# An attention kernel with a written-out step list: five score blocks for queries 0 to 255, longer rows for q and k of group 1, and a new list

## The chip, the cores and the metric

The kernel runs on one core of a Trainium2 chip. The core has five engines that run side by side, each on its own list of instructions in order: TensorE (PE) for matmuls and weight loads, VectorE (DVE), ScalarE (ACT) and GpSimd (POOL) for elementwise work, and SyncE (SP), which here only issues transfers. Sixteen DMA engines move data between main memory and the on-chip memory SBUF. Matmuls write into PSUM, a small memory that the kernel cuts into four slots. The metric is the device time of one execution in microseconds.

## The reference

The input is q, k and v of 8 batches, 8 heads, 576 positions and 64 features. First comes attention in a window: a query sees the keys at most 32 positions away.

```python
scores = scale * np.matmul(q, k.transpose(0, 1, 3, 2))
mask = np.abs(pos[:, None] - pos[None, :]) <= 32
attn = softmax(np.where(mask, scores, -1e9))
x = np.matmul(attn, v)                      # heads side by side: (8, 576, 512)
```

Then comes a mixture of four attention experts on x. A gate picks the two best experts for each row and weighs them. Each expert has its own 64-wide wq, wk, wv and wo; its attention is causal.

```python
logits = x @ w_gate                          # top 2 of 4, softmax over the two
for e in range(4):
    a = causal_softmax(scale * (x @ wq[e]) @ (x @ wk[e]).T)
    out += weight[e] * (a @ (x @ wv[e]) @ wo[e])
```

All inputs and the output are float32.

## The kernel before, in words

A batch is done in two groups of four heads; group g of batch b has the number i = 2b + g, from 0 to 15. The work is cut into steps with names, and the string ORDER lists all of them in the order in which their instructions are issued. Each engine takes its own instructions of this list in that order; waits between engines follow from the data and from the four PSUM slots (the digits behind a colon). The numbers of costs and dependencies in the `step(...)` calls served to find the list; when the kernel is built only the list counts.

The steps are:

- `load.i.kn.n`, `load.i.qn.n` bring k or q of group i to SBUF, in float32: four transfers on SP, one for each head, with rows of 768 B (three positions of 64 features). For group 0 each is cut into two halves (n = 0, 1), and its q goes over ACT's queue (L132). Three buffers of each kind are there, so load i waits for the turn of i - 3.
- `turn.i.kn.n`, `turn.i.qn.n` transpose on DVE in blocks of 32 x 32, six instructions each (L289); features come to lie on partitions, 32 for each head, in two halves.
- `S.i.half` is the window's scores (L305): half 0 for queries 0 to 255, half 1 for 256 to 575. BLK lists the blocks as (first of 64 keys, first query, last query + 1), each done for two feature halves and four heads. ACT then takes the exponential (L310), and a mask product sets what lies outside the window to zero (L312), on DVE for groups 0 and 1 and on POOL for the others. A float32 matmul is two matmuls and two weight loads for PE, so a half with 48 matmuls has 192 PE instructions.
- `loadv.b.n` loads v in pieces that overlap by 64 rows; `dup.b.n.m` copies halves of them on ACT or POOL.
- `U.i.x` and `E.b` multiply by v (L332, L343); DVE divides by the sums (L321, L322). `T.b.g` and `TE.b` transpose the result on PE (L354, L363); ACT copies it out (L357, L364) and POOL makes a bf16 copy (L358, L366).
- `G1.b`, `G3.b` are the gate. `QK.b.j.n`, `V.b.p` are the experts' projections (L425, L441), `PS.b.j.c` the causal scores with exponential and mask (L458, L461, L465), `AV.b.j` the product with v (L482), `PT.b.j` a transpose (L499), `Y.b.t` the output projection (L509), its copy on ACT (L514) and its store on SP (L516, L518).
- `WL.*`, `WC.*` load and cast the weights. `w18:2` means 18 warm-up matmuls into slot 2 (L229), whose result nobody uses; ACT reads one column of it (L230).

The list goes through the groups in a pipeline: scores of later groups stand between the experts' steps of earlier batches. It ends with AV, PT and Y of batches 6 and 7.

Of the kernel before, what the change touches and what calls it, by code (L numbers as in the profile page):

```python
# [19 lines left out]
PE = mybir.EngineType.PE  # L20

ORDER = """
    load.0.kn.0 load.0.qn.0 load.1.qn.0 turn.0.kn.0 loadv.0.0 turn.0.qn.0 load.0.qn.1 late.0 load.1.kn.0
    dup.0.0.0 turn.1.qn.0 dup.0.0.3 load.0.kn.1 w18:2 S.0.0:01 loadv.0.1 turn.0.qn.1 turn.1.kn.0 turn.0.kn.1
    w38:2 S.1.0:10 S.0.1:23 load.2.kn.0 dup.0.0.2 turn.2.kn.0 load.3.qn.0 WL.v load.2.qn.0 w4:1 S.1.1:20
    dup.0.1.3 dup.0.0.1 dup.0.1.2 dup.0.1.0 U.0.1:3 U.0.0:2 dup.0.1.1 WL.q U.1.0:0 U.1.1:3 E.0:2 WC.v
    turn.2.qn.0 T.0.0:0 turn.3.qn.0 T.0.1:3 TE.0:2 w8:1 S.2.0:23 load.3.kn.0 V.0.0:0 G1.0:3 WC.q turn.3.kn.0
    S.2.1:02 QK.0.0.0:1 S.3.0:20 QK.0.0.1:1 loadv.1.0 load.4.kn.0 QK.0.1.0:2 load.4.qn.0 G3.0 dup.1.0.3
    PS.0.0.0:1 dup.1.0.2 V.0.1:0 dup.1.0.0 QK.0.1.1:2 dup.1.0.1 PS.0.0.1:1 S.3.1:03 turn.4.kn.0 U.3.0:2
    turn.4.qn.0 PS.0.0.2:1 U.2.0:0 PS.0.1.0:3 U.2.1:2 load.6.qn.0 S.4.0:31 PS.0.1.1:0 E.1:2 load.5.qn.0  # L30
    U.3.1:3 PS.0.0.3:2 PS.0.1.2:0 turn.5.qn.0 TE.1:1 load.5.kn.0 T.1.0:2 T.1.1:3 turn.5.kn.0 S.4.1:10
    loadv.2.0 AV.0.0:2 PS.0.1.3:3 load.6.kn.0 G1.1:1 turn.6.qn.0 S.5.0:30 QK.1.0.0:2 V.1.0:3 dup.2.0.0 G3.1
    dup.2.0.1 dup.2.0.3 QK.1.1.0:2 dup.2.0.2 QK.1.0.1:0 S.5.1:23 turn.6.kn.0 PS.1.0.0:0 QK.1.1.1:1 loadv.3.0
    V.1.1:2 AV.0.1:3 S.6.0:10 U.4.1:2 load.7.kn.0 dup.3.0.0 U.4.0:1 dup.3.0.2 E.2:0 dup.3.0.1 load.7.qn.0
    PS.1.0.1:2 WL.o PT.0.0:3 turn.7.kn.0 T.2.0:1 dup.3.0.3 turn.7.qn.0 S.6.1:30 U.5.1:2 PS.1.1.0:3
    load.8.qn.0 PS.1.0.2:1 U.5.0:0 S.7.0:23 TE.2:1 T.2.1:0 load.8.kn.0 load.9.qn.0 turn.8.qn.0 PS.1.1.1:2
    U.6.0:3 U.6.1:1 WC.o PS.1.0.3:2 PS.1.1.2:0 turn.8.kn.0 G1.2:3 S.7.1:12 G3.2 QK.2.0.0:0 V.2.0:1
    turn.9.qn.0 PS.1.1.3:0 S.8.0:32 loadv.4.0 QK.2.0.1:0 dup.4.0.0 QK.2.1.0:3 load.10.qn.0 U.7.1:2 E.3:3
    dup.4.0.1 U.7.0:0 dup.4.0.3 load.9.kn.0 dup.4.0.2 turn.9.kn.0 PS.2.0.0:2 S.8.1:31 load.11.kn.0 V.2.1:0
    load.10.kn.0 QK.2.1.1:2 PS.2.0.1:3 S.9.0:10 load.11.qn.0 PT.0.1:2 AV.1.0:3 TE.3:2 turn.10.qn.0  # L40
    PS.2.0.2:0 Y.0.0:1 T.3.0:2 turn.10.kn.0 S.9.1:30 PS.2.1.0:1 AV.1.1:2 T.3.1:3 U.8.1:0 load.13.qn.0
    PS.2.1.1:1 turn.11.qn.0 PS.2.0.3:2 G1.3:3 S.10.0:01 load.13.kn.0 QK.3.0.0:2 PT.1.0:0 load.12.kn.0 G3.3
    Y.0.2:1 QK.3.0.1:2 turn.11.kn.0 PS.2.1.2:0 S.10.1:13 V.3.0:2 PS.2.1.3:3 PS.3.0.0:1 U.8.0:0 E.4:3
    load.12.qn.0 PS.3.0.1:1 loadv.5.0 turn.12.qn.0 V.3.1:2 QK.3.1.0:0 S.11.0:13 turn.12.kn.0 QK.3.1.1:0
    AV.2.0:1 Y.0.4:3 PS.3.0.2:2 U.9.0:0 dup.5.0.2 dup.5.0.3 U.9.1:3 S.11.1:12 PT.1.1:3 T.4.1:0 AV.2.1:3
    load.14.kn.0 TE.4:2 T.4.0:1 PT.2.0:2 Y.1.0:0 PS.3.0.3:3 PS.3.1.0:1 G1.4:2 S.12.0:30 G3.4 QK.4.0.0:1
    Y.1.2:3 PT.2.1:0 dup.5.0.0 QK.4.0.1:1 dup.5.0.1 AV.3.0:0 PS.3.1.1:3 PS.4.0.0:1 V.4.0:2 PS.3.1.2:0
    PS.4.0.1:1 U.11.0:3 U.11.1:0 loadv.6.0 U.10.0:1 E.5:3 U.10.1:0 PS.3.1.3:1 PS.4.0.2:3 Y.1.4:2 Y.2.0:1
    V.4.1:3 turn.13.qn.0 QK.4.1.0:2 S.12.1:13 PS.4.0.3:2 QK.4.1.1:0 Y.2.2:1 PT.3.0:2 TE.5:0 turn.13.kn.0
    load.14.qn.0 T.5.0:3 AV.3.1:1 T.5.1:0 PS.4.1.0:3 AV.4.0:2 loadv.7.0 turn.14.kn.0 S.13.0:10 dup.6.0.3  # L50
    QK.5.0.0:3 PS.4.1.1:1 Y.2.4:0 PT.3.1:2 QK.5.0.1:3 PS.4.1.2:2 turn.14.qn.0 load.15.qn.0 S.13.1:01 Y.3.0:3
    V.5.0:2 PS.4.1.3:3 dup.6.0.1 PS.5.0.0:1 dup.6.0.0 G1.5:0 S.14.0:23 QK.5.1.0:1 G3.5 dup.6.0.2 V.5.1:2
    Y.3.2:3 QK.5.1.1:1 PS.5.0.1:2 dup.7.0.1 AV.4.1:0 PS.5.1.0:1 PS.5.0.2:2 U.12.0:3 dup.7.0.0 U.13.1:1
    load.15.kn.0 E.6:2 U.13.0:3 U.12.1:1 PS.5.0.3:2 PS.5.1.1:0 TE.6:3 T.6.1:2 PT.4.0:1 turn.15.kn.0 T.6.0:0
    PS.5.1.2:1 S.14.1:23 dup.7.0.2 turn.15.qn.0 AV.5.0:0 QK.6.0.0:1 PT.4.1:3 V.6.0:2 PS.5.1.3:3 S.15.0:10
    Y.3.4:3 QK.6.1.0:2 QK.6.0.1:0 dup.7.0.3 V.6.1:2 QK.6.1.1:3 PS.6.0.0:0 S.15.1:21 G1.6:3 PS.6.1.0:2
    PS.6.0.1:0 U.14.0:1 U.14.1:2 U.15.0:0 G3.6 U.15.1:1 E.7:2 PS.6.0.2:0 Y.4.0:3 T.7.0:1 TE.7:0 T.7.1:2
    PT.5.0:3 AV.5.1:1 PS.6.1.1:3 PS.6.0.3:0 G1.7:2 PS.6.1.2:3 Y.4.2:0 G3.7 QK.7.0.0:1 AV.6.0:3 PS.6.1.3:0
    QK.7.0.1:1 QK.7.1.0:0 Y.4.4:3 PT.5.1:2 PS.7.0.0:1 QK.7.1.1:0 Y.5.0:2 PS.7.0.1:1 PS.7.1.0:0 V.7.0:3
    PS.7.0.2:1 PT.6.0:2 AV.6.1:0 PS.7.1.1:3 Y.5.2:2 PS.7.0.3:1 PS.7.1.2:3 V.7.1:0 PT.6.1:2 AV.7.0:0  # L60
    PS.7.1.3:2 Y.5.4:3 AV.7.1:0 Y.6.0:3 PT.7.0:2 PT.7.1:2 Y.7.0:2 Y.6.2:0 Y.7.2:0 Y.6.4:2 Y.7.4:2
"""


MASKS = ["DVE"] * 2 + ["POOL"] * 14
DUP = ["ACT", "POOL", "ACT", "POOL"]

S = 576
# [6 lines left out]
def kernel(  # L75
# [43 lines left out]
    def parts(i):  # L119
        return [(0, 3), (3, 6)] if i < 1 else [(0, 6)]  # L120

    def load(b, g, nm, n):

        src = {"kn": k, "qn": q}[nm]
        if n == 0:
            nat[nm, b, g] = natp.tile([128, 6, 3, 64], F32, name=nm, tag=nm)
        t = nat[nm, b, g]
        i = 2 * b + g
        a0, a1 = parts(i)[n]
        eng = nc.scalar if i == 0 and nm == "qn" else nc.sync  # L130
        for hh in range(4):
            eng.dma_start(t[32 * hh:32 * hh + 32, a0:a1, :, :].rearrange("p a s d -> p a (s d)"),  # L132
                          src[b, 4 * g + hh].rearrange("(a p s) d -> p a (s d)", p=32, s=3)[:, a0:a1])


# [124 lines left out]
    def cast_weights(n):  # L260
# [4 lines left out]
        else:  # L265
# [2 lines left out]

    BLK = [[[(128, 64, 192), (64, 0, 128)], [(0, 0, 64), (192, 128, 192)], [(256, 192, 256), (192, 192, 256)]],
           [[(384, 320, 448), (320, 256, 384)], [(512, 448, 576), (448, 384, 512)],
            [(256, 256, 320), (576, 512, 576)]]]
    CUT = [0, 256, 576]
# [5 lines left out]
    def turn(b, g, nm, n):  # L280
        if n == 0:
            qt_[b, g, nm] = (KTS[(2 * b + g) % 2][:, :, 32:608] if nm == "kn" else
                             qkt.tile([128, 2, S], F32, name="T" + nm, tag="T" + nm))
        T = qt_[b, g, nm]
        n_ = nat[nm, b, g]
        a0, a1 = parts(2 * b + g)[n]
        for dh in range(2):
            for x in range(3):
                nc.vector.transpose(T[:, dh, :].rearrange("q (a p s) -> q s a p", p=32, s=3)[:, x, a0:a1],  # L289
                                    n_[:, a0:a1, x, 32 * dh:32 * dh + 32])  # L290

    def win_scores(b, g, half):
        QT, KT = qt_[b, g, "qn"], KTS[(2 * b + g) % 2]
# [234 lines left out]
    def step(name, fn, pe, after, ops=(), slots=()):  # L528
        steps[name] = dict(fn=fn, pe=pe, after=list(after), ops=list(ops), slots=list(slots))

    for b in range(B):
        for g in range(2):
            i = 2 * b + g
            np_ = len(parts(i))
            for nm in ("kn", "qn"):
                for n, (a0, a1) in enumerate(parts(i)):
                    step(("load", i, nm, n), lambda b=b, g=g, nm=nm, n=n: load(b, g, nm, n), 0,
                         [("turn", i - 3, nm, m) for m in range(len(parts(i - 3)))] if i > 2 else
                         [("load", i, nm, 0)] if n else [],
                         [("AQ" if i == 0 and nm == "qn" else "SP", 1.8, -1), ("DMA", 2.3 * (a1 - a0) / 6, 0),  # L540
                          ("LAT", 0.8, 1)])
                    step(("turn", i, nm, n), lambda b=b, g=g, nm=nm, n=n: turn(b, g, nm, n), 0,
                         [("load", i, nm, n)] + ([("turn", i, nm, 0)] if n else []) +
                         ([("S", i - 2, 1)] if i > 1 else []), [("DVE", 0.3 + 1.3 * (a1 - a0) / 6, -1)])
            mk = ("DVE", 0.62) if MASKS[i] == "DVE" else ("POOL", 1.25)
            for half in range(2):
                step(("S", i, half), lambda b=b, g=g, half=half: win_scores(b, g, half), (0.9, 1.1)[half],
                     [("turn", i, nm, n) for nm in ("kn", "qn") for n in range(np_ if half else 1)] + ([("S", i, 0)] if half else []) +
                     ([("U", i - 3, 0), ("U", i - 3, 1), ("E", (i - 3) // 2)] if i > 2 else []),
                     [("ACT", (0.5, 0.6)[half], -1), (*mk, 0), ("ACT", (0.5, 0.6)[half], -1), (*mk, 2)], (0, 2))  # L550
# [114 lines left out]
```

## Time and profile before

| what | value |
|---|---|
| median of 13 runs | 269.7 us (266.84 to 274.45) |
| profiled execution, time | 267.08 us |
| profiled execution, span from first to last instruction | 265.4 us |
| PE busy | 238.6 us (90%), 5940 matmuls, 5940 weight loads |
| DVE, ACT, POOL busy | 171.1, 160.3, 147.5 us |
| mean granted PE clock | 0.993 |
| moved by DMA | 40.72 MB, mean 153 GB/s |
| warm-up matmuls | 68 in four steps (18, 38, 4, 8), PE busy 19.1 us |

The profile names lines of the kernel before with L. In a row of the timeline stand the start in us, the length, the engine, the line, the operation, what it writes and reads, the tile's shape and a count, since neighbours of one kind are merged; in brackets stands how long the engine had been idle before it, and what ended that idle time. "issue" means that nothing in the profile ended it. The row of the DMA queue gives the number of packets, their megabytes and their share of the 16 DMA engines' time; the queue named "instruction" on q8 brings the PE's own instructions. Busy PE time is modelled at its ends, so I go by the starts of steps where a step's length matters.

### The profile page before, as it was taken

Reading aid. Unit: us, or ns where it says so; the run is one execution under the profiler, and the core shown is the slowest. Engines: PE = TensorE matmul, PEld = TensorE weight load, DVE = VectorE, ACT = ScalarE, POOL = GpSimd, SP = SyncE. Lnnn points to the kernel's source line nnn. Section 1 sums busy time; section 2 is a strip of 40 time slices with the busy share of each in tenths; the row PEclk is TensorE's granted clock in tenths of the full one; section 3 lists DMA queues with packets and bytes.
Section 4 is the critical chain, followed back from the end, with each engine's and each line's share of the span. In section 5 each row is a group of like instructions: output and inputs, shape, how many; then the busy total and the mean of one; then the engine's idle time right before and its main releaser. Section 6 shows DMA issues by size and latency. Waiting matters only on the chain. (4 is left out here: it accounts for less than half of the span.)

```text
span 265.4 us, 13457 instructions
## 1 busy us (share of the span) xinstructions
PE 238.6 (90%) x5940; PEld 182.9 (69%) x5940; DVE 171.1 (64%) x538; ACT 160.3 (60%) x247; POOL 147.5 (56%) x202
## 2 busy tenths in 40 slices
PE   7598698988879989878999999999999999999752
PEld 2345686777768778766878877787679878876520
DVE  7554786476757948656968756768558846574530
ACT  1304536677455966556775668577796845867543
POOL 8102035966965997649674775267972974521300
PEclk9989999999999999999999999999999999999999
DMA  6989889999999769941889525639836010223227
GB/s 161 214 181 200 184 198 201 227 211 192 196 213 223 165 143 205 205 84 40 226 214 197 141 84 137 129 101 236 204 103 172 2 25 2 82 83 103 99 111 245
DMA packets 76570, 40.72 MB, mean 153 GB/s; under 512 B 47072, under 2 KB 71648, under 8 KB 76512
## 3 DMA queue, kind: packets, MB, share of 16 engines
q1 hardware_dynamic: 75616, 39.28, 65.2%
q8 instruction: 46, 0.75, 1.3%
q10 hardware_dynamic: 896, 0.59, 0.9%
q14 instruction: 12, 0.10, 0.2%
HBM read 30.42 MB, written 9.44 MB: 150 GB/s over the span
## 5 line engine op out<-in xcount | busy, mean ns | idle before, releaser
L312 POOL TENSOR_TENSOR AT<-AT,MASKP 128x512 f32<-128x512 f32 (+1 forms) x56 | 77.7, 1409 | 38.3 <-ACT AT L310 38.1
L461 ACT ACTIVATE ATE<-ps 128x1024 bf16<-128x1024 f32 (+1 forms) x64 | 52.0, 836 | 22.5 <-PE ps L458 22.1
L310 ACT ACTIVATE AT<-sc 128x512 f32<-128x512 f32 (+1 forms) x64 | 38.2, 650 | 33.7 <-PE sc L305 33.7
L305 PE MATMUL sc<-Tqn,KT 32*64 32x128 f32 (+1 forms) x3072 | 49.5, 255 | 4.4 <-issue 4.0
L305 PEld LDWEIGHTS sc<-Tqn,KT 32*64 32x64 f32 x3072 | 44.0, 130 | 12.3 <-issue 8.4
L332 PE MATMUL u<-VS,AT 128*64 128x65 f32 x1024 | 35.3, 224 | 3.9 <-issue 3.7
L332 PEld LDWEIGHTS u<-VS,AT 128*64 128x64 f32 x1024 | 32.3, 138 | 7.1 <-issue 5.9
L289 DVE STREAM_TRANSPOSE Tqn<-qn 128x192 f32<-128x192 f32 (+1 forms) x102 | 29.0, 392 | 3.1 <-DMA qn<-in_q_dram 3.1
L289 DVE STREAM_TRANSPOSE KT<-kn 128x192 f32<-128x192 f32 (+1 forms) x102 | 29.1, 393 | 2.5 <-DMA kn<-in_k_dram 2.5
L465 POOL TENSOR_SCALAR_AFFINE_SELECT ATE<-ATE 128x384 bf16<-128x384 bf16 x32 | 15.9, 521 | 25.4 <-ACT ATE L461 25.3
L514 ACT COPY ysb<-py 128x1024 f32<-128x1024 f32 (+1 forms) x24 | 20.5, 867 | 10.8 <-PE py L509 8.9
L322 DVE TENSOR_TENSOR XN<-u,rs 128x512 f32<-128x512 f32 (+1 forms) x40 | 25.5, 638 | 1.4
L358 POOL CAST XTB<-XTF 128x512 bf16<-128x512 f32 x32 | 18.6, 614 | 13.9 <-ACT XTF L357 13.7
L161 POOL COPY VS<-VS 64x1024 f32<-64x1024 f32 (+1 forms) x18 | 16.9, 940 | 14.4 <-DMA VS<-in_v_dram 13.8
L509 PE MATMUL py<-WO,OTT 128*128 128x512 bf16 x80 | 20.8, 380 | 2.9 <-ACT ysb L514 2.4
L229 PE MATMUL warm<-WARM 128*128 128x512 bf16 x68 | 19.1, 445 | 4.1 <-ACT wsink L230 2.7
L425 PE MATMUL pp<-XTB,WQ 128*128 128x288 bf16 x128 | 18.7, 287 | 2.4 <-issue 2.4
L357 ACT COPY XTF<-tx 128x512 f32<-128x512 f32 x32 | 17.0, 595 | 6.0 <-PE tx L354 5.6
L441 PE MATMUL pv<-WV,XTB 128*128 128x256 bf16 x160 | 20.1, 273 | 0.2 <-DVE OE L491 0.2
L432 DVE CAST QKE<-pp 128x576 bf16<-128x576 f32 x16 | 12.0, 753 | 12.5 <-PE pp L425 12.5
L458 PE MATMUL ps<-QKE 64*128 64x64 bf16 (+4 forms) x192 | 19.7, 279 | 0.1
L159 ACT COPY VS<-VS 64x1024 f32<-64x1024 f32 (+1 forms) x18 | 17.1, 948 | 3.9 <-DMA VS<-in_v_dram 3.6
(77 smaller groups left out, 314.1 us busy)
## 6 DMA issues: line engine op xcount, KB each, us to landing
qn<-in_q_dram SPq DMA_DIRECT2D x60, 144.0 KB, 4.8
kn<-in_k_dram SPq DMA_DIRECT2D x60, 144.0 KB, 5.0
out_dram<-ysb SPq DMA_DIRECT2D x16, 512.0 KB, 3.1
VS<-in_v_dram SPq DMA_DIRECT2D x21, 256.0 KB, 5.8
VS<-in_v_dram SPq DMA_DIRECT2D x14, 192.0 KB, 5.5
out_dram<-ysb SPq DMA_DIRECT2D x8, 128.0 KB, 2.3
VS<-in_v_dram SPq DMA_DIRECT2D x6, 128.0 KB, 3.3
qn<-in_q_dram ACTq DMA_DIRECT2D x8, 72.0 KB, 3.0
```

What stands on the lines that cost most here:

```text
L229: nc.tensor.matmul(w, WARM[:, 0:128], WARM, start=True, stop=True)
L289: nc.vector.transpose(T[:, dh, :].rearrange("q (a p s) -> q s a p", p=32, s=3)[:, x, a0:a1], n_[:, a0:a1, x, 32 * dh:32 * dh + 32])
L305: nc.tensor.matmul(sl[hh // 2][p0:p0 + 64, hh % 2, lo - c0:hi - c0], KT[r, dh, k0:k0 + 64], QT[r, dh, lo:hi], start=(dh == 0), stop=(dh == ...
L310: nc.scalar.activation(ap, sl[p][:, :, 0:c1 - c0], EXP, scale=scale_att)
L312: eng.tensor_tensor(out=ap, in0=ap, in1=MASK[:, None, c0:c1].to_broadcast([128, 2, c1 - c0]), op=MULT)
L322: nc.vector.tensor_tensor(out=o, in0=u[:, :, :, 0:64], in1=rs[:, :, :, None].to_broadcast([128, n, 4, 64]), op=MULT)
L332: nc.tensor.matmul(us[64 * y:64 * y + 64, t, 65 * hh:65 * hh + 65], A[:, hh, 64 * a:64 * a + 64], V[:, a, 4 * g + hh, 0:65], start=True, s ...
L441: nc.tensor.matmul(o, XTB[:, dt, 128 * t:128 * t + 128], WV[:, dt, :], start=(dt == 0), stop=(dt == NDT - 1))
L458: nc.tensor.matmul(ps[:, eo, at:at + hi - lo], QKE[r, 1, 128 * kt:128 * kt + 128], QKE[r, 0, lo:hi], start=True, stop=True)
L461: nc.scalar.activation(ATE[0:rows, :, 512 * c:512 * c + w], ps[0:rows, :, 0:w], EXP, scale=scale_moe)
L509: nc.tensor.matmul(py[:, t - t0, :], OTT[:, j, 128 * t:128 * t + 128], WO[:, j, :], start=(j == 0), stop=(j == 1))
L514: nc.scalar.copy(ysb[0:n, 0:m, :], py[0:n, 0:m, :])
```

## The change

Three things are changed at once. First, half 0 of the scores has five blocks of keys: the block of keys 192 to 255 took queries 128 to 191 and, apart from them, 192 to 255; now it takes queries 128 to 255 in one. That makes 40 matmuls instead of 48, over the same columns.

```diff
-    BLK = [[[(128, 64, 192), (64, 0, 128)], [(0, 0, 64), (192, 128, 192)], [(256, 192, 256), (192, 192, 256)]],
+    BLK = [[[(128, 64, 192), (64, 0, 128)], [(0, 0, 64), (192, 128, 256)], [(256, 192, 256)]],
```

Second, group 1 loads q and k with one transfer each on SP: a partition gets 18 neighbouring positions of a head, 4608 B in a row. The turn then is two transposes of 128x576 instead of six of 128x192.

```diff
+LONG = range(1, 2)
...
-            nat[nm, b, g] = natp.tile([128, 6, 3, 64], F32, name=nm, tag=nm)
+            nat[nm, b, g] = natp.tile([128, 18, 64], F32, name=nm, tag=nm)
...
+        if i in LONG:
+            nc.sync.dma_start(t, src[b, 4 * g:4 * g + 4].rearrange("h (p s) d -> (h p) s d", s=18))
+            return
...
+            if 2 * b + g in LONG:
+                nc.vector.transpose(T[:, dh, :].rearrange("q (p s) -> q s p", s=18), n_[:, :, 32 * dh:32 * dh + 32])
+                continue
```

Third, the whole list ORDER is another one; it came from a model of the engines that also counts fetches of 256 instructions. The steps are the same but for the warm-ups: 33 in six steps (18, 3, 1, 3, 1, 7) instead of 68 in four. Its beginning, before and after, and some later places of the new one:

```diff
-    load.0.kn.0 load.0.qn.0 load.1.qn.0 turn.0.kn.0 loadv.0.0 turn.0.qn.0 load.0.qn.1 late.0 load.1.kn.0
-    dup.0.0.0 turn.1.qn.0 dup.0.0.3 load.0.kn.1 w18:2 S.0.0:01 loadv.0.1 turn.0.qn.1 turn.1.kn.0 turn.0.kn.1
-    w38:2 S.1.0:10 S.0.1:23 load.2.kn.0 dup.0.0.2 turn.2.kn.0 load.3.qn.0 WL.v load.2.qn.0 w4:1 S.1.1:20
-    dup.0.1.3 dup.0.0.1 dup.0.1.2 dup.0.1.0 U.0.1:3 U.0.0:2 dup.0.1.1 WL.q U.1.0:0 U.1.1:3 E.0:2 WC.v
-    turn.2.qn.0 T.0.0:0 turn.3.qn.0 T.0.1:3 TE.0:2 w8:1 S.2.0:23 load.3.kn.0 V.0.0:0 G1.0:3 WC.q turn.3.kn.0
-    S.2.1:02 QK.0.0.0:1 S.3.0:20 QK.0.0.1:1 loadv.1.0 load.4.kn.0 QK.0.1.0:2 load.4.qn.0 G3.0 dup.1.0.3
+    load.1.kn.0 load.0.qn.0 load.0.kn.0 load.1.qn.0 load.0.qn.1 turn.0.qn.0 turn.1.kn.0 turn.0.kn.0
+    turn.1.qn.0 w18:3 S.0.0:01 loadv.0.0 turn.0.qn.1 load.0.kn.1 dup.0.0.1 dup.0.0.2 turn.0.kn.1 dup.0.0.3
+    dup.0.0.0 w3:3 S.1.0:02 U.0.0:1 S.0.1:20 load.2.kn.0 loadv.0.1 load.2.qn.0 late.0 dup.0.1.1 dup.0.1.3
+    S.1.1:31 turn.2.kn.0 dup.0.1.0 dup.0.1.2 w1:2 U.0.1:0 WL.q w3:2 U.1.0:1 WL.v E.0:3 load.3.qn.0 U.1.1:2
+    T.0.0:0 w1:1 T.0.1:2 turn.2.qn.0 load.3.kn.0 TE.0:0 loadv.1.0 S.2.0:31 w7:0 G1.0:1 turn.3.qn.0
+    turn.3.kn.0 WC.q QK.0.0.0:3 G3.0 load.4.qn.0 S.2.1:02 QK.0.1.0:3 WC.v QK.0.0.1:0 S.3.0:32 PS.0.0.0:0
...
+    load.6.kn.0 turn.5.kn.0 S.4.1:03 AV.0.0:1 dup.2.0.1 QK.1.0.0:2 V.1.0:3 load.8.kn.0 turn.6.qn.0
...
+    S.7.0:01 dup.3.0.3 load.9.kn.0 dup.3.0.2 loadv.4.0 turn.8.qn.0 AV.1.0:2 Y.0.0:3 load.11.kn.0 QK.2.0.0:1
+    V.2.1:0 turn.9.kn.0 G1.2:2 PS.2.0.0:0 S.8.0:13 QK.2.1.1:0 G3.2 PS.2.0.1:1 load.9.qn.0 U.6.1:3 U.6.0:0
...
+    PT.1.1:2 AV.2.0:0 PS.2.1.2:3 S.9.0:12 turn.10.qn.0 V.3.0:3 Y.0.4:2 QK.3.0.0:1 PS.2.1.3:2 S.10.0:30
+    S.9.1:21 PT.2.0:0 QK.3.0.1:3 loadv.5.0 G1.3:0 PS.3.0.0:3 QK.3.1.0:1 dup.4.0.3 G3.3 Y.1.0:2 V.3.1:3
...
+    G1.5:0 S.13.0:23 G3.5 AV.4.0:1 QK.5.0.0:2 load.15.qn.0 load.15.kn.0 Y.2.2:3 V.5.0:0 PS.4.1.3:3 S.12.1:12
...
+    dup.7.0.0 dup.7.0.3 PS.5.1.3:0 PS.6.0.0:1 V.6.0:2 Y.3.4:3 QK.6.1.0:1 PS.6.0.1:3 S.15.1:20 S.14.1:31
```

So load.8.kn, load.9.kn and load.11.kn now come ahead of load.9.qn. The last eight steps, from Y.6.0 to Y.7.4, stand in the order that they had.

## The prediction

> **What bounds the kernel now.** I read three views in this order: busy time by stretch, the timeline around TensorE's (PE's) gaps, and the page's list of DMA queues. The stretches (window, length, then busy us and instruction count of PE, weight loads, DVE, ACT, POOL; last the granted clock, the DMA share, GB/s):
>
> ```profile
> 10.00:15.00 5.00, 3.42 (x10) 1.29 (x10) 3.87 (x14) 1.77 (x4) 0.17 (x1) 0.74 1.07 198
> 28.36:44.63 16.27, 14.46 (x415) 12.30 (x410) 11.49 (x32) 9.09 (x17) 5.13 (x7) 1.00 0.98 198
> 44.63:116.00 71.37, 63.23 (x1921) 51.95 (x1917) 49.69 (x157) 45.55 (x69) 52.93 (x58) 1.00 0.98 197
> 116.00:248.66 132.66, 130.57 (x3110) 102.91 (x3110) 88.50 (x274) 93.17 (x139) 79.35 (x107) 1.00 0.45 117
> ```
>
> From 28 to 249 us PE is the bound. Its steps stand back to back, and what idle time remains is "issue", a wait for nothing that the profile shows. Until 116 us the DMA engines are full too (0.98): a second limit right behind the first. The start is different:
>
> ```profile
> 9.80 1.75 DVE L289 STREAM_TRANSPOSE Tqn<-qn 128x192 f32<-128x192 f32 x6 [2.15 <-DMA qn<-in_q_dram]
> 11.59 10.05 PE L229 MATMUL warm<-WARM 128*128 128x512 bf16 x38 [2.74 <-ACT wsink L230]
> 16.75 2.69 DVE L289 STREAM_TRANSPOSE KT<-kn 128x192 f32<-128x192 f32 x12 [2.37 <-DMA kn<-in_k_dram]
> 21.56 2.75 PE L305 MATMUL sc<-Tqn,KT 32*64 32x128 f32 x192
> ...
> 113.29 1.35 PE L305 MATMUL sc<-Tqn,KT 32*64 32x128 f32 x82
> 115.99 0.37 PE L305 MATMUL sc<-Tqn,KT 32*64 32x64 f32 x14 [1.35 <-issue]
> ```
>
> Here the reader sees that S.1.0 starts only at 21.56: load.1.kn lands at 16.7, and the 38 warm-ups, which themselves waited 2.74 us for their slot, run until 21.6. The last two rows show one score step cut in two by a gap. Its cause:
>
> ```profile
> q8 instruction: 46, 0.75, 1.3%
> ```
>
> The page has 5940 matmuls and 5940 weight loads; 46 fetches make some 256 instructions each. I counted: every such gap stands a multiple of 256 PE instructions from the others. Where 256 instructions are used up in less than about 4.4 us PE stands still until the next block is there (26.91 to 31.28, 111.54 to 115.99); a score step has 192 in 1.4 us. From 44.6 us on these gaps add up to 13.5 us: 8.0 until 97 us, 3.7 until 121, 1.8 later, where a block takes some 3.9 us (DMA 0.45).
>
> **Part 1, the start.** The first stretch is one chain, redone for the new order. DVE starts turns at 5.4, as before, since its memsets end then. Six 96-column transposes take 1.1 us, six of 192 columns 1.75. The two 128x576 ones of a long row are not in the trace: as many elements as six of 192, so from 1.5 (per-column slope of the two rows) to 2.5 (6 x 0.41, the mean of one); I take 2.0. Rows of 4608 B aren't there either: between the rate of 768 B packets (median 51 ns on 16 engines, 240 GB/s) and of 2048 B ones (85 ns, 385 GB/s); I take the longer rows, so 1.18 MB go in 3.1 us instead of 4.9. turn.0.qn.0 ends at 6.5, turn.1.kn 8.5, turn.0.kn.0 9.6: S.0.0 runs at 9.6, 2.2 later than now. turn.1.qn ends at 11.6: S.1.0 at 11.7, not 21.6. Masks (1.3) and both half-turns of block 0 (1.1 each) put S.0.1 at 15.4, the DVE's U.0.0 puts S.1.1 at 17.6; S.1.1 crosses a fetch boundary 4.4 us after the one in S.0.1 and ends at 21.0, against 28.4. U.0.1, w3, U.1.0, E.0, U.1.1 and one more fetch wait: 25.6. T.0.0, T.0.1 (behind 0.9 us of DVE), TE to 28; S.2.0 behind turn.2.qn on DVE, 28.5 to 29.7; w7 1.7, G1.0 1.2; QK.0.0.0 waits for four 0.63 us casts on ACT, which stand behind S.2.0's exponentials: 33.4, against 44.6. V.0.0 (1.85) and S.2.1 (1.48), done by then in the old order, are still owed: 44.6 - 33.4 - 3.3 = **7.9 us** gained. The warm-ups (68 to 33) are worth nothing beyond this: they only filled that wait.
>
> Against it: fewer warm-ups. After 2.8 us of idle PE the clock row above is 0.74, and warm-ups stand 0.425 us apart for a while, then half that. The Trainium skill, "TensorE: Matmul & The Clock Gate", Part 1, says that one idle window of about 3.4 us halves the clock until an equally long busy one. By the rule PE, with waits of 1 to 3 us between short steps until 17.6, could stay at half speed to about 21 us; by the row the cold time was 3.4 us once. Most of the cold work lies under DVE waits; on the path are S.1.1 and U.0.1. Cost 0 to 2.5; I take 1.0. The start then gains **6.9**.
>
> **Part 2, five blocks.** Half 0 has 40 matmuls instead of 48, that is 160 PE instructions, not 192; columns stay 512 per head. A half 0 step takes 1.38 us, half 1 with the same 192 instructions and 640 columns 1.48: so 128 columns cost 0.10, the rest is per instruction: (1.38 - 0.40)/192 = 5.1 ns, times 32 = **0.16 us**. Bounds 0 and 1.38/6 = 0.23. Thirteen such steps lie after QK.0.0.0: six before S.9.0 (1.0), seven after (1.1). ACT and masks are untouched.
>
> **Part 3, the order against the fetches.** I laid the new list on blocks of 256 with the step times of this trace. Blocks under 4.4 us up to about 97 us lack 6.4 us (8.0 measured): 1.6 gained; to 121 us 2.0 (3.7): 1.7 gained. Later it places dense steps together, S.10.0 with S.9.1 (a block of 1.96 us), AV.4.0 with S.13.0 (2.88), S.15.1 with S.14.1 (2.16): at 3.9 us a block, 6.5 missing against 1.8 measured: 4.7 lost. After 97 us the net is **3.0 lost**. The skill's "Runtime: NRT & Kernel Launch", Instruction fetch mechanics, speaks against the whole part: it calls the crossing of a block "mostly hidden", since instructions issue slower than blocks arrive. By the rule this term is 0; the rows (1.35 us idle inside one step) decide against it.
>
> **Part 4, the second limit.** Up to 97 us PE would be ahead by 6.9 + 1.0 + 1.6 = 9.5 us, but the transfers must keep pace. All that goes up to load.4 (q, k, v and weights, 9.8 MB) passes at 197 GB/s from 1.7 us: 51.6 now, 49.8 with the 1.8 us of the long rows. With 1.3 us from landing to the turn (the least that rows show in the start), and 1.8 for the turn, S.4.0 can't run before 52.9; now it is at 59.1, with 0.6 us less to do ahead of it in the new list. So the gain there is at most 5.6, and a blocked turn blocks DVE's copies behind it, and so PE's slots. I take **6.0**: 3.5 are lost to loads. SP's list is moved too: load.8.kn, 9.kn and 11.kn now stand ahead of load.9.qn; by the same sum (19.8 MB ahead of it, at 197 GB/s) it lands at about 105, some 9 us before S.9.0 needs its turn, so it costs nothing more.
>
> **Sum.** 6.0 (up to 97 us) + 1.1 - 3.0 = 4.1 us. The end (AV.7.0 to the last store, 17 us, waits on DVE and ACT) keeps its order: 0. Profiled execution 267.1 -> 263.0; it lies 2.6 under the median of 269.7, so the median goes to **265.6 us**.
>
> **Rivals.** (a) The loads keep pace, because landings now have more slack than the single rows show (load.6.qn and load.3.qn are turned 12 to 18 us after landing): 9.5 + 1.1 - 3.0 = 7.6, 262.1 us. For it: DVE waited for no load after 17 us. (b) The long rows are no faster and the loads leave a gain of 3 only: 3 + 1.1 - 3.0 = 1.1, 268.6 us, no change. For it: DMA 0.98 in the stretch. (c) Slower: fetches. With PE pressed closer against full queues each block takes 4.7 us, also late: the new list then lacks 24.7 us, 11.2 more than the 13.5 measured, of which at most 3.5 lie under load waits: 7.6 - 11.2 = -3.6, 273.3 us. It decides from about 4.5 us a block at the late boundaries. For it: single blocks took 4.9 (to 74.3 us); against: with DMA at 0.45 three stalled ones took 3.8 to 4.3. (d) That it doesn't do what it says is out: the changed list has 40 matmuls in half 0 and single DMAs for load.1.
>
> **Numbers.** Forecast 0.45, (a) 0.27, (b) 0.13, (c) 0.15. A measurement tells 0.5% (1.3 us) from no change. Forecast and (a) are faster but for a twentieth: faster 0.73, same 0.13, slower 0.14. Range: unknown costs (clock 0 to 2.5, blocks 0 to 0.23 each, loads 0 to 3.5) reach from 260 to 269; with part of (c) 259.5 to 270.5.
>
> **What would show it.** S.1.0 at 12 us and QK.0.0.0 near 33 confirm part 1; score steps of half 0 at 1.22 us part 2; gaps inside S.9.1, AV.4.0 and S.14.1 part 3; DVE waiting for kn and qn between 45 and 70 us part 4. Wrong: S.1.0 after 16 us, clock under 1 past 25 us, or more than 20 us of issue gaps.

## The result, and the profile after

The changed kernel takes 264.64 us (median of 11 runs, 263.07 to 270.56); the kernel before, run again beside it, 270.57 us (48 runs). The ratio is **0.9843, 95% interval 0.9807 to 0.9878**: 4.2 us faster (3.3 to 5.2), where 4.1 were forecast. Both kernels have some runs that are several us slower, at a lower granted clock (0.969 against 0.981 on average for the changed kernel); the ratio leaves them out, so it shows less than the two medians. The profiled execution of the changed kernel took 266.54 us (span 264.8), above its median, while that of the kernel before (267.08) lies below its own. So the two traces together show 0.6 us of the gain; they tell where time went, not how much was won.

The same stretches of the changed kernel (columns as before):

```profile
10.00:15.00 5.00, 4.18 (x136) 2.89 (x143) 4.64 (x13) 1.92 (x4) 0.77 (x1) 0.66 1.24 220
28.36:44.63 16.27, 14.76 (x380) 10.95 (x377) 9.83 (x35) 10.19 (x21) 8.29 (x10) 1.00 0.96 191
44.63:116.00 71.37, 64.05 (x1777) 52.04 (x1776) 50.16 (x154) 47.28 (x69) 51.32 (x59) 0.98 0.98 203
116.00:248.66 132.66, 126.51 (x2949) 100.29 (x2948) 86.06 (x268) 88.97 (x134) 78.61 (x106) 1.00 0.45 112
```

The reader is to see the last row: after 116 us PE was busy for 130.57 us of 132.66 before, now for 126.51. It idles 4 us more in a stretch where the DMA engines are busy for only 0.45. In the rows of 28 to 116 us it idles a little less. The start, from the timeline:

```profile
0.80 0.40 SPq L133 DMA_DIRECT2D kn<-in_k_dram  x1
1.26 5.28 SPq L138 DMA_DIRECT2D kn<-in_k_dram  x4
...
8.06 2.30 DVE L295 STREAM_TRANSPOSE KT<-kn 128x576 f32<-128x576 f32 x2
11.51 2.34 DVE L295 STREAM_TRANSPOSE Tqn<-qn 128x576 f32<-128x576 f32 x2 [0.26 <-DMA qn<-in_q_dram]
...
10.82 2.16 PE L314 MATMUL sc<-Tqn,KT 32*64 32x128 f32 x80 [2.50 <-DVE KT L298]
14.22 1.33 PE L314 MATMUL sc<-Tqn,KT 32*64 32x128 f32 x80
...
22.42 1.03 PE L314 MATMUL sc<-Tqn,KT 32*64 32x128 f32 x56 [1.09 <-issue]
```

S.1.0 now runs at 14.22 instead of 21.56, and the step QK.0.0.0 at 36.04 instead of 44.63. It is a real gain, but 2.6 us less than forecast. And two of the gaps of the later part:

```profile
62.08 0.87 PE L491 MATMUL po<-VE,ATE 128*128 128x65 bf16 x23
64.82 0.39 PE L491 MATMUL po<-VE,ATE 128*128 128x65 bf16 x7 [1.87 <-issue]
...
127.78 2.31 PE L314 MATMUL sc<-Tqn,KT 32*64 32x128 f32 x150
131.86 0.47 PE L314 MATMUL sc<-Tqn,KT 32*64 32x64 f32 x26 [1.76 <-issue]
```

AV.0.0 and S.9.1 are cut in two, with "issue" as the reason. Between the two cuts lie 3328 records of PE, its semaphore waits counted in: 13 x 256. So these are instructions that are not there yet. q8 has two fetches fewer than before:

```profile
q8 instruction: 44, 0.72, 1.3%
```

I count such gaps in every trace in one way: the time from one weight load's start to the next right at a multiple of 256 PE instructions (the same multiples as before), where it is over 0.3 us, less the 0.05 us that lie between any two, and without the last 20 us, where PE waits for other engines.

### The profile page after: what moved, and what is told of

Read it like the earlier page. It is cut to its first block, busy times and chain, and to the rows that moved or that the text cites. A ratio compares the mean times of both kernels' runs of the same rounds, so it can differ in the third digit from the quotient of the medians.

```text
span 264.8 us, 12861 instructions
## 1 busy us (share of the span) xinstructions
PE 232.3 (88%) x5649; PEld 179.6 (68%) x5649; DVE 171.6 (65%) x530; ACT 161.5 (61%) x249; POOL 148.6 (56%) x202
## 5 line engine op out<-in xcount | busy, mean ns | idle before, releaser
L314 PE MATMUL sc<-Tqn,KT 32*64 32x128 f32 (+1 forms) x2816 | 49.0, 265 | 10.8 <-DVE KT L298 5.1
L314 PEld LDWEIGHTS sc<-Tqn,KT 32*64 32x64 f32 x2816 | 43.1, 132 | 18.8 <-issue 9.7
L341 PE MATMUL u<-VS,AT 128*64 128x65 f32 x1024 | 35.9, 224 | 4.3 <-issue 3.3
L298 DVE STREAM_TRANSPOSE Tqn<-qn 128x192 f32<-128x192 f32 (+1 forms) x96 | 27.4, 387 | 4.1 <-DMA qn<-in_q_dram 2.2
L523 ACT COPY ysb<-py 128x1024 f32<-128x1024 f32 (+1 forms) x24 | 20.6, 869 | 14.4 <-PE py L518 12.2
L298 DVE STREAM_TRANSPOSE KT<-kn 128x192 f32<-128x192 f32 (+1 forms) x96 | 27.5, 391 | 1.1 <-DMA kn<-in_k_dram 1.0
L474 POOL TENSOR_SCALAR_AFFINE_SELECT ATE<-ATE 128x384 bf16<-128x384 bf16 x32 | 15.9, 521 | 18.9 <-ACT ATE L470 18.7
L167 POOL COPY VS<-VS 64x1024 f32<-64x1024 f32 (+1 forms) x18 | 17.7, 986 | 12.8 <-DMA VS<-in_v_dram 12.3
L367 POOL CAST XTB<-XTF 128x512 bf16<-128x512 f32 x32 | 18.5, 614 | 11.3 <-ACT XTF L366 11.3
L491 PE MATMUL po<-VE,ATE 128*128 128x65 bf16 x480 | 18.2, 193 | 4.8 <-issue 3.0
L450 PE MATMUL pv<-WV,XTB 128*128 128x256 bf16 x160 | 21.1, 281 | 0.1
L491 PEld LDWEIGHTS <-ATE 128*128 128x128 bf16 x480 | 16.2, 97 | 7.2 <-issue 6.9
L441 DVE CAST QKE<-pp 128x576 bf16<-128x576 f32 x16 | 12.1, 754 | 10.8 <-PE pp L434 10.7
```

What stands on the lines that cost most here:

```text
L314: nc.tensor.matmul(sl[hh // 2][p0:p0 + 64, hh % 2, lo - c0:hi - c0], KT[r, dh, k0:k0 + 64], QT[r, dh, lo:hi], start=(dh == 0), stop=(dh == ...
L341: nc.tensor.matmul(us[64 * y:64 * y + 64, t, 65 * hh:65 * hh + 65], A[:, hh, 64 * a:64 * a + 64], V[:, a, 4 * g + hh, 0:65], start=True, s ...
L450: nc.tensor.matmul(o, XTB[:, dt, 128 * t:128 * t + 128], WV[:, dt, :], start=(dt == 0), stop=(dt == NDT - 1))
L491: nc.tensor.matmul(po[:, eo, 65 * qt:65 * qt + 65], ATE[:, eo, o:o + 128], VE[:, kt, 2 * j + eo, :], start=(kt == 0), stop=(kt == qt))
L523: nc.scalar.copy(ysb[0:n, 0:m, :], py[0:n, 0:m, :])
```

## The experiments

All kernels ran beside the kernel before on the same chip. Ratios are to it; the gaps are those of the one profiled execution, in us.

| kernel | ratio (95% interval) | gaps to 44 us | 44 to 118 | after 118 |
|---|---|---|---|---|
| before | 1 | 3.5 | 10.8 | 3.0 |
| changed | 0.9843 (0.9807 to 0.9878) | 1.4 | 8.0 | 7.1 |
| changed, again | 0.9881 (0.9790 to 0.9972) | 1.3 | 6.5 | 7.0 |
| new list alone | 0.9991 (0.9953 to 1.0029) | 2.1 | 9.3 | 6.6 |
| five blocks alone | 0.9853 (0.9772 to 0.9934) | 3.4 | 10.2 | 3.6 |
| five blocks alone, again | 0.9900 (0.9834 to 0.9965) | 2.3 | 11.3 | 2.5 |
| changed without long rows | 0.9896 (0.9848 to 0.9944) | 1.1 | 7.2 | 5.7 |
| changed, shifted by 128 | 0.9859 (0.9796 to 0.9922) | 4.5 | 8.1 | 6.0 |
| changed, few transfers | 0.9436 (0.9367 to 0.9505) | 1.7 | 3.1 | 3.7 |
| before, few transfers | 0.9574 (0.9463 to 0.9686) | 4.3 | 5.1 | 0.9 |
| changed, long rows 1 to 7 | 0.9771 (0.9699 to 0.9844) | 1.9 | 5.4 | 6.9 |
| changed, k of group 0 first | 0.9809 (0.9718 to 0.9901) | 1.3 | 8.0 | 6.0 |
| long rows 1 to 15, k of 0 first | 0.9938 (0.9870 to 1.0007) | 1.9 | 8.3 | 6.5 |
| long rows 1 to 7, k of 0 first, shifted by 64 | 0.9776 (0.9714 to 0.9839) | 2.6 | 7.5 | 1.0 |

### Each part alone

The new list alone is the changed kernel with six blocks and short rows:

```diff
-LONG = range(1, 2)
+LONG = range(0, 0)
...
-    BLK = [[[(128, 64, 192), (64, 0, 128)], [(0, 0, 64), (192, 128, 256)], [(256, 192, 256)]],
+    BLK = [[[(128, 64, 192), (64, 0, 128)], [(0, 0, 64), (192, 128, 192)], [(256, 192, 256), (192, 192, 256)]],
```

> The new list alone, with six blocks and rows of 768 B for group 1. My theory (the list brings the start, five blocks 0.12 us for each of 16 half 0 steps, long rows next to nothing): 2 us under the kernel before (between 1 and 3.5). S.1.0 starts by 15 us. Laid on blocks of 256 instructions, at 4.4 us a block early and 3.9 late, the list lacks 12.0 us early and 6.9 late, against 14.0 and 2.8 in the kernel before. Rival A (the long rows brought the start): no faster than before. Rival B (the list brings all of it, five blocks and long rows nothing): 4.2 us under.

Measured: 0.2 us (a ratio of 0.9991), from 1.3 us faster to 0.8 slower. S.1.0 starts at 14.33, so the start is the new one without any long row, and still nothing of it arrives. That is nearest to rival A's time, but not for its reason. The trace shows one place where it went:

```profile
57.17 1.30 PE L314 MATMUL sc<-Tqn,KT 32*64 32x128 f32 x85
61.22 0.36 PE L314 MATMUL sc<-Tqn,KT 32*64 32x64 f32 x11 [2.75 <-issue]
```

This is S.4.0. Its q and k were turned by 55.9, its first 85 matmuls have run, and PE stands for 2.75 us in the middle of it. With six blocks the list's gaps sum to 15.9 us from 44 us on (13.8 before). Another place is the clock. It stood at half right behind this gap, and once more from 44.9 to 48.3 us; in the trace of the kernel before it is at 1.00 from 16 to 260 us:

```profile
62.00:65.30 3.30, 3.30 (x50) 2.77 (x45) 1.78 (x6) 1.61 (x4) 2.74 (x3) 0.50 1.00 198
```

The runs that the ratio counts have a mean granted clock of 0.973, those of the kernel before beside them 0.988. That is worth up to 4 us (0.015 x 268, an estimate), less where PE waits anyway. How the missing gain divides between gaps, clock and loads isn't shown.

Five blocks alone is the kernel before with the BLK line of the change.

> Five blocks alone in the kernel before, with its list and its rows. My theory: 0.12 us for each half 0 step, 1.6 us in all behind the start, and boundaries of 256 instructions that move because 32 instructions fewer stand in each such step (blocks lack 11.3 us early and 2.6 late, against 14.0 and 2.8): 3 us under the kernel before (between 1.5 and 4.5). Rival A (transfers are the bound until 116 us, so only steps later than that count): 0.9 us under. Rival B (the time is set by the columns alone, not by instructions): no change.

> Five blocks alone in the kernel before, once more, since its first interval (0.977 to 0.993) doesn't tell 2 us from 4. My theory now (0.12 us for each of 16 half 0 steps, and fetch gaps as long as before): 2 us under the kernel before, 1.5 to 2.5 us above the changed kernel. Rival A (five blocks are the whole gain, list and long rows nothing): within 0.8 us of the changed kernel, 4 us under the kernel before. Rival B (boundaries moved by fewer instructions add a gain of their own): 3 us under.

Measured: 0.9853 and, again, 0.9900. Weighted by their intervals that makes 0.988, give or take 0.005: 3.2 us faster (1.8 to 4.6). The steps themselves give 16 x 0.12 = 1.9 of it. The gaps in its two traces (13.8 and 13.8 us from 44 us on) are those of the kernel before, so a gain from moved boundaries, which my first expectation and rival B of the second counted on, isn't there: the 3 us of that expectation were met by luck. Rival A can't be told from my theory by these intervals. What is clear is the ranking: five blocks alone are as fast as the changed kernel within the measurement (the changed kernel's two comparisons, weighted alike, give 0.985), and the list alone isn't. The length of a step is read from its start to the next one's, first in the kernel before, then in the changed one:

```profile
46.59 1.44 PE L305 MATMUL sc<-Tqn,KT 32*64 32x128 f32 x96
47.97 1.15 PE L425 MATMUL pp<-XTB,WK 128*128 128x288 bf16 x8
...
123.12 1.33 PE L314 MATMUL sc<-Tqn,KT 32*64 32x128 f32 x80
124.38 1.92 PE L450 MATMUL pv<-WV,XTB 128*128 128x256 bf16 x16
```

It was 1.38 us and is 1.26.

Without long rows only the first of the two edits above is made.

> The changed kernel with group 1 in rows of 768 B again. The PE's instruction stream is the same to the last instruction, so the boundaries of 256 stay. My theory (the long rows move their bytes faster, but SP's issues behind them were held up from 1.8 to 5.3 us, and the turns are longer): within 1 us of the changed kernel, so 3.2 to 5.2 us under the kernel before. Rival A (my prediction: 1.8 us of transfer time saved for everything behind): 2 us slower than the changed kernel. Rival B (the held-up issues cost more than the rows gain): 1.5 us faster than the changed kernel.

Measured: 0.9896 against 0.9843, a difference of 1.4 us with an uncertainty of 1.6: my theory and rival A both lie inside. The start shows why it is small. The long q is turned from 11.51 us on instead of 12.74, but the two long turns take 2.30 and 2.34 us instead of about 1.75 each. S.1.0 starts at 13.94 without long rows and at 14.22 with them, and the step behind it at 15.88 and 15.48. In one point my expectation was wrong: SP's issues are held up with short rows too (its first eight take 6.89 us), so long rows are not the cause.

### Are the gaps tied to the boundaries?

The shift puts more, narrower warm-ups into the idle time ahead of S.0.0 (`w18`), and so moves every later step by 128 PE instructions:

```diff
-        for _ in range(n):
-            nc.tensor.matmul(w, WARM[:, 0:128], WARM, start=True, stop=True)
+        n, c = (82, 112) if n == 18 else (n, 512)
+        for _ in range(n):
+            nc.tensor.matmul(w[:, 0:c], WARM[:, 0:128], WARM[:, 0:c], start=True, stop=True)
```

> The changed kernel with its first 18 warm-ups of 512 columns replaced by 82 of 112 columns: about as many columns, 128 PE instructions more, all in the idle time before S.0.0. Every later step stands 128 instructions further on in the blocks of 256. My theory (late gaps come from dense steps that lie between two boundaries): the late blocks lack 3.7 us instead of 8.3, the early ones 11.3 instead of 9.3: 2.5 us under the changed kernel (between 1 and 4), and the gaps in S.9.1 and AV.4.0 are gone, with one in S.14.1 instead. Rival A (the gaps belong to steps or to waits and not to boundaries): same gaps, same time as the changed kernel. Rival B (what fetches give, loads take): gaps move, time within 0.7 us of the changed kernel.

```profile
128.70 2.65 PE L315 MATMUL sc<-Tqn,KT 32*64 32x128 f32 x176
...
212.24 2.91 PE L315 MATMUL sc<-Tqn,KT 32*64 32x128 f32 x189
216.99 0.33 PE L315 MATMUL sc<-Tqn,KT 32*64 32x64 f32 x3 [1.84 <-issue]
```

S.10.0 with S.9.1 now runs through, 176 matmuls in one; S.15.1 with S.14.1 is cut three matmuls before its end. The places are as expected, and rival A falls: nothing of these steps changed but their position. The size was not: 14.1 us of gaps from 44 us on against 15.1, and 3.1 more in the start, and no difference in time (0.9859 against 0.9843). Rival B's time, though no load took the gain: other blocks simply lack as much, and the time doesn't show the 3.1 us of the start either. Laying the list on blocks with usual step times placed these gaps well and got their sum wrong.

### What do the transfers cost?

Both kernels without the q and k of groups 3 to 15:

```diff
+        if 2 * b + g > 2:
+            nat[nm, b, g] = nat[nm, (2 * b + g - 3) // 2, (2 * b + g - 3) % 2]
+            return
```

> The changed kernel without the transfers of q and k of groups 3 to 15, 15.3 MB of 40.7 (those groups' turns read what groups 0 to 2 left in the three buffers, so their scores are computed from the q and k of groups 0 to 2; every instruction of PE, DVE, ACT and POOL stays). My theory (fetches of instructions eat the gain of the start, loads only slow each fetch a little): fetch gaps between 44 and 118 us fall from 7.8 to about 5, other waits hardly, and it is 2 to 3 us under the changed kernel: 6.5 us under the kernel before. Rival A (my prediction's second limit, loads took 3.5 us of the start's gain): 4.5 us or more under the changed kernel. Rival B (loads cost nothing at all): within 1 us of the changed kernel.

> The kernel before without the same transfers of q and k of groups 3 to 15 (scores of those groups from the q and k of groups 0 to 2). My theory: fetch gaps between 44 and 118 us fall from 10.1 to about 8, so 2 to 3 us under the kernel before, and the changed kernel without them stays 4 us below this one. Rival A (loads hold the changed kernel only): within 1 us of the kernel before, and 7.5 us above the changed kernel without them.

Measured: 15.2 us under the kernel before and 11.5 us under it. Every number of mine was too small, for both kernels. The changed kernel with few transfers:

```profile
44.63:116.00 71.37, 68.67 (x1978) 57.65 (x1977) 57.11 (x179) 52.60 (x78) 55.72 (x68) 1.00 0.25 63
116.00:248.66 132.66, 122.10 (x2779) 95.39 (x2792) 82.63 (x257) 87.98 (x130) 73.03 (x97) 1.00 0.31 90
```

and the kernel before with few transfers, in the first of these stretches:

```profile
44.63:116.00 71.37, 67.58 (x2157) 55.82 (x2147) 52.32 (x166) 49.17 (x76) 56.74 (x62) 1.00 0.22 48
```

The DMA share falls from 0.98 to 0.25 and 0.22, and PE works for some 4.5 us more in the same 71 us. Most of it is fetches: from 44 us on the gaps fall from 15.1 to 6.8 us in the changed kernel and from 13.8 to 6.0 in the kernel before, that is by **8 us in each**. Queues full of q and k make the PE's own instructions late. The fetches' packets on q8 show a part of it: in this stretch one took 1.30 us on average in the changed kernel, 1.05 with few transfers (1.24 and 1.09 in the kernel before). Much of the rest of the changed kernel's gain is its waits for loads. Its DVE and PE around 40 us:

```profile
38.52 1.81 DVE L298 STREAM_TRANSPOSE Tqn<-qn 128x192 f32<-128x192 f32 x6 [0.54 <-DMA qn<-in_q_dram]
40.90 1.77 DVE L298 STREAM_TRANSPOSE KT<-kn 128x192 f32<-128x192 f32 x6 [0.57 <-DMA kn<-in_k_dram]
...
42.02 0.48 PE L314 MATMUL sc<-Tqn,KT 32*64 32x128 f32 x16 [1.28 <-DVE KT L298]
...
50.38 1.83 DVE L298 STREAM_TRANSPOSE Tqn<-qn 128x192 f32<-128x192 f32 x6 [1.68 <-DMA qn<-in_q_dram]
53.12 1.15 PE L341 MATMUL u<-VS,AT 128*64 128x65 f32 x32 [0.86 <-DVE XN L331]
```

The first turns are those of group 3, the last is that of q of group 4; behind it DVE's XN is late, and PE waits. The same turns of group 3 with few transfers wait for nothing:

```profile
37.27 1.79 DVE L301 STREAM_TRANSPOSE Tqn<-qn 128x192 f32<-128x192 f32 x6
38.95 1.75 DVE L301 STREAM_TRANSPOSE KT<-kn 128x192 f32<-128x192 f32 x6
```

To sum such waits I take stretches of the list that have the clock at 1.00. From QK.0.0.0 to AV.0.0, without a fetch gap, the changed kernel takes 26.04 us (25.25 in its second trace), and 23.37 with few transfers. So the new order pays **1.9 to 2.7 us for loads** there. The kernel before takes 14.4 us from QK.0.0.0 to S.4.0, and 13.7 with few transfers; without the gaps in it (2.2 and 1.2 us) that is 12.2 and 12.5: it pays nothing. So of its 11.5 us some 3.7 are not explained; its trace with few transfers is of an execution of 261.32 us, where the runs that the ratio counts took 257.02 and 258.31. Yet the two kernels with few transfers differ by a ratio of 0.986 (0.9436 / 0.9574), give or take 0.014, no more than with all transfers: the kernel before had as much to win from quiet queues.

Long rows for more groups cut the number of packets instead of the bytes:

```diff
-LONG = range(1, 2)
+LONG = range(1, 8)
```

> The changed kernel with rows of 4608 B for groups 1 to 7 instead of group 1 alone. Each turn is two transposes of 1.16 us instead of six of 0.30, 0.55 us more on DVE, 12 more of them, 6.6 us of DVE time in all; the transfers of 7.1 MB take about half as long. My theory (loads are no limit, DVE has slack in most of these places, quieter queues bring fetches a little earlier): within 1.5 us of the changed kernel, with a DMA share well under 0.9 from 28 to 100 us. Rival A (loads are the limit): 3 us faster than the changed kernel. Rival B (a longer turn blocks the copies behind it on DVE and so PE's slots): 2 to 4 us slower than the changed kernel.

Measured: 0.9771, 6.2 us under the kernel before; against the changed kernel's 0.9843 that is 2 us, give or take 2.2. The DMA share from 44 to 116 us falls from 0.98 to 0.78, the gaps of 44 to 118 us from 8.0 to 5.4, and 6.6 us more of DVE's work hurt nothing. Rival B falls; my bound of 1.5 us and rival A's 3 both lie within that uncertainty.

The start with k of group 0 first, on SP and on DVE:

```diff
-    load.1.kn.0 load.0.qn.0 load.0.kn.0 load.1.qn.0 load.0.qn.1 turn.0.qn.0 turn.1.kn.0 turn.0.kn.0
+    load.0.kn.0 load.0.qn.0 load.1.kn.0 load.1.qn.0 load.0.qn.1 turn.0.kn.0 turn.0.qn.0 turn.1.kn.0
```

> The changed kernel with the first steps in another order: load.0.kn.0 ahead of load.1.kn.0 on SP, and turn.0.kn.0 ahead of turn.0.qn.0 and turn.1.kn.0 on DVE. My theory (the chain of the start is transfers into turns on DVE, and q of group 0 landed too late to be turned first): turns start at 5.4 us instead of 7.1, S.0.0 runs at 8 instead of 10.8, S.1.0 at 12.6 instead of 14.2, S.1.1 some 1 us earlier; of this at most 1 us is left at the end: 0 to 1 us under the changed kernel. Rival (q of group 0 or k of group 1 lands later in this order, and S.1.0 waits): S.1.0 at 14 us or later, no gain.

```profile
9.03 2.34 DVE L295 STREAM_TRANSPOSE KT<-kn 128x576 f32<-128x576 f32 x2 [1.70 <-DMA kn<-in_k_dram]
12.02 2.34 DVE L295 STREAM_TRANSPOSE Tqn<-qn 128x576 f32<-128x576 f32 x2 [0.66 <-DMA qn<-in_q_dram]
```

S.0.0 runs at 7.53, as expected, but now DVE waits 1.70 and 0.66 us for k and q of group 1, and most of S.1.0 runs at 14.4. The rival was right. The transfers, not the order of the turns, set S.1.0. The time, 0.9809, is not to be told from the changed kernel's.

### Does a version beat both?

> The changed kernel itself, beside the other three. All theories: 4 us under the kernel before (ratio 0.981 to 0.988 as in its first comparison). It is there as the yardstick of the other three.

> The changed kernel with rows of 4608 B for groups 1 to 15 and k of group 0 first. Theory (transfers lengthen fetches and hold turns everywhere; without q and k of groups 3 to 15 fetch gaps after 118 us fell from 7.1 to 3.7): fetch gaps after 118 us fall below 5.5, before it below 5.5 as with groups 1 to 7, and it is 1 to 2 us under the kernel with long rows for groups 1 to 7: 7 to 8 us under the kernel before. Rival (DVE, 0.55 us more for each of 28 turns, 15 us in all, becomes late for PE's slots after 116 us, where PE stands on nothing else): 4 us under the kernel before or less.

> The changed kernel with rows of 4608 B for groups 1 to 7, k of group 0 first, and the first 18 warm-ups in 50 of 184 columns, so that later steps stand 64 PE instructions further on in the blocks of 256. Theory (gaps follow boundaries, and at this place the late dense steps lack less): gaps after 118 us fall from 6.9 (long rows for groups 1 to 7) to about 4.5, none of 2 us in S.9.1; 8 us under the kernel before. Rival (a shift only moves gaps, as the one by 128 did: 14.9 us from 44 us on against 15.1): 6 us under, as with the long rows alone.

The edits are those shown: `LONG = range(1, 16)` or `range(1, 8)`, the other order at the start, and in the last one `(50, 184)` in place of `(82, 112)`. The changed kernel gave 0.9881 this time. With long rows everywhere it fell back to 0.9938. This is the rival's outcome; its trace has gaps hardly shorter (8.3 and 6.5, where both were expected below 5.5). The 6.5 count in one of 1.94 us at 191 us, for which the profile names ACT's exponential, though it stands at a boundary too. Whether DVE is behind the loss stays open.

The last kernel has fewer late gaps than expected: after 118 us 1.0 us is left of 6.9 (some 4.5 were forecast), and S.9.1 runs in one piece.

```profile
128.26 2.66 PE L315 MATMUL sc<-Tqn,KT 32*64 32x128 f32 x176
```

Its time, 262.53 us (ratio 0.9776, 6.0 us under the kernel before), is the rival's: equal to the long rows alone, which kept 6.9 us of late gaps. In its trace 2.1 us of gaps came back before 118 us and 0.7 in the start. Both kernels with long rows for groups 1 to 7 have a median below the changed kernel's; against its 0.985 the last one is 2 us faster, give or take 1.9, so it beats the kernel before clearly and the changed one only just.

## Why the prediction came out right, point by point

**The sum was right, in part by luck.** The terms of list and long rows came to 2.0 us (4.1 less 2.1 for five blocks). The list alone brought 0.2, give or take 1.0, and list and long rows on top of five blocks 0.9, give or take 1.7 (0.985 against 0.988). Five blocks were put at 2.1 and brought 3.2, give or take 1.4. So the parts may be off by 1 us each, in opposite directions; the intervals allow the forecast too. The traces show the terms one by one, in us:

| term | forecast | first trace | second trace |
|---|---|---|---|
| start, up to QK.0.0.0 | 7.9 - 1.0 (clock) | 5.3 | 4.8 |
| five blocks behind it | 2.1 | 1.6 | 1.6 |
| gaps from 44 to 118 us, and later | 3.3 - 4.7 | 2.8 - 4.1 | 4.3 - 4.0 |
| waits for loads | -3.5 | -2.7 | -1.9 |
| half clock after the start | 0 | -1.7 | -1.5 |
| sum | 4.1 | 1.2 | 3.3 |
| difference of the spans | | 0.6 | 2.6 |

The columns compare two traces of the changed kernel with the one of the kernel before; their terms give the difference of the spans within 0.7 us. The start was put some 2 us too high and the clock behind it was left out, while loads took less than forecast. That all runs together still gave the 4.1 can't be read from these traces, as that of the kernel before lies under its median.

**What bounds the kernel.** PE, its fetches, and full queues right behind: shown. But I treated the queues as a limit on loads alone. Those transfers cost each kernel 8 us through the fetches, and the new order some 2 to 3 us more through loads.

**Part 1, the start: 7.9 forecast, 5.3 measured** (44.63 - 36.04 - 3.3). The step that failed is "DVE starts turns at 5.4, as before": the first turn started at 7.06. DVE's memsets did end by 5.2, but the new list turns q of group 0 first, and that q landed at 6.9 us instead of 5.6, though ACT issued its four transfers at the same times as before: now 0.59 MB of load.1.kn go beside them. With k of group 0 ahead of it the first turn started at 5.26. SP's four issues for load.0.kn.0 took 5.28 us instead of 1.82, which held back load.1.qn. A smaller share is the price of a long turn, 2.3 us and not 2.0. The clock was at half speed from 10.66 to 14.07 us, mostly beside waits, as assumed.

**Part 2: 0.12 us for each step, not 0.16**, 1.6 instead of 2.1 for the 13 steps counted. That five blocks alone brought more than 1.9 isn't explained; the intervals would allow it to be chance.

**Part 3, the order against the fetches: right in the sum.** Up to 97 us the gaps fell from 8.0 to 6.2 (forecast 6.4), to 121 us from 3.7 to 1.8 (forecast 2.0), and later they rose from 2.0 to 7.1 (forecast 1.8 to 6.5). Of the three places named S.9.1 has its gap in all seven traces with these boundaries (1.9 to 2.3 us, so counted); AV.4.0 has 0.3, S.14.1 none. U.9.0, AV.3.0, G1.4 and U.10.1 have the others. The Trainium skill, "Runtime: NRT & Kernel Launch", Instruction fetch mechanics, calls the crossing of a block mostly hidden; here the shifted kernels show that PE's gaps follow the boundaries.

**Part 4, loads take 3.5 us: shown in kind.** Waits that go away with the transfers are 1.9 to 2.7 us. They stand at 38 to 53 us rather than at 45 to 70. The cap at S.4.0 was there: q of group 4 was waited for until 50.38, and S.4.0 ran at 54.25 (52.9 was the earliest by the forecast). But as much was lost before it, to the turns of group 3, which the forecast didn't have.

**The end** moved by nothing: from AV.7.0 to the last instruction 17.7 us before (247.65 to 265.4) and 17.6 after (247.16 to 264.8).

One sign that was named as telling against the forecast did appear, a clock under 1 after 25 us: in the profiled execution it stood at 0.50 from 65.30 to 68.70, right behind the gap in AV.0.0. The two steps there (QK.1.0.0 and V.1.0) took 4.49 us instead of 2.82 in the second trace: 1.7 us. The prediction had a price for the clock in the start alone; the last section has more on it.

The rivals: (a), loads keep pace, is out, as S.3.0's waits show and a gain of at most 5.2 us, where it had 7.6. (b), loads leave a gain of 3 only, describes the list well but not the total. (c), slower fetches, had the mechanism (stalled late blocks took 3.7 to 5.2 us, not 3.9), but not the size. In the forecast's chances the 0.73 for "faster" doesn't follow: 0.45 and 0.27, less a twentieth, are 0.68.

## What to carry to other kernels

When PE is bound by the delivery of its own instructions, every edit that changes how many instructions stand ahead of a step re-deals the gaps, so compare one part alone and a shifted version before a part gets the credit. Instructions taken out of a bound engine's stream are worth more than a shorter start that later limits take back (here some 3.2 us against 0.2). And where queues are full, fewer packets shorten the fetch gaps too (8.0 to 5.4 us here), whether or not a load is late.

## What the runs showed that I had not expected

- Fetches are late when data moves: taking 15.3 MB of transfers away shortened PE's gaps by 8 us in both kernels. Yet with few transfers the block that ends in S.9.1 still took 3.8 us, as with all of them.
- A fetch gap can cost twice. The same stretch of two executions of the changed kernel, first the one whose gap in AV.0.0 left PE idle for 1.87 us:

```profile
65.30:68.70 3.40, 3.40 (x18) 2.30 (x16) 1.68 (x6) 0.64 (x1) 2.64 (x3) 0.50 1.10 212
```

and then the second one, where that gap left it idle for 1.04 us:

```profile
65.30:68.70 3.40, 3.40 (x102) 2.85 (x100) 2.47 (x8) 1.19 (x3) 2.67 (x3) 1.00 1.05 214
```

The granted clock is 0.50 in the one and 1.00 in the other. But length alone doesn't decide. The gap in S.9.1 left PE idle for 1.76 us in the first execution and halved nothing; in the changed kernel without long rows it was 1.75 us, and behind it stands this:

```profile
131.40:134.70 3.30, 3.30 (x31) 2.02 (x32) 1.22 (x2) 1.09 (x2) 2.73 (x2) 0.50 0.64 142
```

And in the new list alone an idle time of 2.82 us at 121.6 us halved nothing. What does decide stays open.
- Two transposes of 128x576 take 2.3 us, six of 128x192 over as many elements 1.75.
